# One of three on-chip copies of remainder weights moves from ScalarE to VectorE, and ScalarE's part of the start-up waits for it

## The chip, the cores and the metric

The kernel runs on one core of one Trainium2 chip. Its engines are TensorE (PE in the profile; PEld is its weight load), VectorE (DVE), ScalarE (ACT), GpSimd (POOL) and SyncE (SP). The metric is the device time of one execution in microseconds (us), lower is better.

## The reference

Six cross layers of a recommender network, in bf16, with x0 of 4096 rows and 416 columns, ws of 6 matrices of 416 by 416, and bs of 6 biases:

```
x = x0
for l in range(ws.shape[0]):
    x = x0 * (x @ ws[l] + bs[l]) + x
return x
```

## The kernel before, in words

**Layout.** The state is kept transposed: the 416 columns lie on partitions, the 4096 rows of x0 along the free dimension. 416 is 3 times 128 and a remainder of 32. The three full blocks are in `XM` (three buffers, `XM[0]` holds x0), the remainder in `XR`, where four groups of 512 rows (g = 0 to 3) are stacked on four groups of 32 partitions. The 4096 rows are two halves (s = 0, 1) of four such groups. `WM` holds the weights of the full blocks, `WR` the 32 remainder rows of each layer's weights, copied four times onto the four partition groups, since a matrix product with 32 rows of `XR` needs its weights on the same partitions.

**Loading.** x0 comes from HBM in eight transposing DMAs of 512 rows each, `load_x0t(s, g)` (line 77), all issued by SP one behind another. I call those of the first half T0 to T3. The remainder columns of x0 come as short rows of 64 bytes into `xrem` in four loads (line 82): SP issues the one for s = 0, partitions 0 to 63, between T1 and T2; ACT issues the one for s = 0, partitions 64 to 127 (I call it R), and later the one for s = 1, partitions 0 to 63 (R'). ACT also issues the load of the first layer's `WM` and the load that puts the remainder weights of layers 0 and 1 on partitions 0 to 31 of `WR` (line 85). The three other partition groups of `WR` are filled by on-chip copies: DVE makes those of layer 0 (line 113), ACT those of layer 1 (line 115). The weights of layer 1 in `WR` are first read by `mm_row(1, ...)` (line 214), at the end of the first layer.

**The remainder.** `x0_rem` (lines 160 to 167) turns `xrem` into `XR[0]`: DVE transposes in two parts (line 164), ACT copies the first part into place and DVE the second (line 165), and DVE makes a copy with the two 32-row groups swapped, `XRx` (line 167). For s = 0 this is done for partitions 0 to 63 first, and for partitions 64 to 127 later, behind the first element-wise work (line 272).

**The order of the work.** Every engine executes its instructions in the order in which the program writes them; waits are on semaphores. `first_layer(0)` has PE multiply group g = 0 for the three column blocks (9 matmuls on T0's data), then g = 1 (9 matmuls on T1), then the remainder rows (line 254, 6 matmuls), then g = 2 (9 on T2) and g = 3 (9 on T3), and again remainder rows, which need partitions 64 to 127 of `XR`. Products land in PSUM, whose eight banks are handed out in pairs (`two_banks`); ACT and DVE (lines 189 and 190, 172 and 180) read them out and form the next state. Layers 1 to 4 follow in the loop at line 359, and the last layer produces output rows directly (lines 397 to 457).

The lines that the change touches are 114 and 115; what stands next in ACT's queue is R, and behind it the copy at line 165 and the load R'.

Of the kernel before, what the change touches and what calls it, by code (L numbers as in the profile page):

```python
# [16 lines left out]
def kernel(  # L17
# [7 lines left out]
    nc = tc.nc  # L25
# [7 lines left out]
    NG = 4  # L33
# [20 lines left out]
    WR = const.tile([P, L, D], BF16)  # L54
# [20 lines left out]
    def load_x0t(s, g):  # L75
        c0 = col0(s, g)
        nc.sync.dma_start_transpose(out=XM[0][:, :, c0:c0 + CW], in_=x0[c0:c0 + CW, 0:NK * P])
# [33 lines left out]
        nc.gpsimd.tensor_copy(bsb[32 * g:32 * g + 32, :], bsb[0:R, :])  # L111
    for g in range(1, NG):
        nc.vector.tensor_copy(WR[32 * g:32 * g + 32, 0, :], WR[0:32, 0, :])
    for g in range(1, NG):
        nc.scalar.copy(WR[32 * g:32 * g + 32, 1, :], WR[0:32, 1, :])
    load_x0t(0, 1)
    load_xrem(nc.sync, 0, 0, 64)
    load_xrem(nc.scalar, 0, 64, 128)
# [369 lines left out]
```

## Time and profile before

| quantity | value |
|---|---|
| median of 3 runs | 130.51 us (130.41 to 130.77) |
| profiled execution | 130.41 us |
| its span in the profile | 128.6 us |
| PE busy | 122.5 us, 95% |
| DVE busy | 105.4 us, 82% |
| ACT busy | 84.9 us, 66% |
| POOL busy | 8.9 us, 7% |
| granted TensorE clock | 0.998 of full speed |

The span is the stretch from the first to the last recorded work; 1.8 us of the profiled execution's time lie outside it. Times in the profile are counted from the start of the span. In the timeline a row gives start, duration, engine, source line, operation, output and input, shape and count, and in brackets how long the engine sat idle before and what released it; rows of ACTq and SPq are DMAs being issued by ACT and SP. Waits are given as the total, the number and the longest. In the DMA view a queue's line gives packets, megabytes, and the time that its packets took as a share of 16 DMA engines in the chosen stretch; overlapping packets can bring it over 100%. q1 is the queue of SP's DMAs, q10 that of ACT's.

### The profile page before, as it was taken

The page shows a single profiled execution, that of the slowest core. Times are in us where ns is not written, and L with a number is a line of the kernel's source. Part 1 is how long each engine was busy: PE and PEld are TensorE (multiplying, and loading weights), DVE is VectorE, ACT ScalarE, POOL GpSimd, SP SyncE. Part 2 cuts the span into 40 slices and gives each one's busy share as a digit, 9 for nine tenths or more (in the row PEclk, how much of TensorE's full clock was granted, in tenths as well). Part 3 has the DMA queues.
Part 4 walks back from the last instruction along what each step waited for, and adds up shares of the span by engine and source line. Part 5 has one row for each costly group of instructions (what it writes and reads, how often), then busy time and mean ns, then how long its engine had stood idle before and what let it go on. Part 6 is the DMA issues. An engine that isn't in the chain of part 4 may idle for free. (4 is left out here: it accounts for less than half of the span.)

```text
span 128.6 us, 4040 instructions
## 1 busy us (share of the span) xinstructions
PE 122.5 (95%) x1731; PEld 54.9 (43%) x1731; DVE 105.4 (82%) x192; ACT 84.9 (66%) x97; POOL 8.9 (7%) x29
## 2 busy tenths in 40 slices
PE   6998999999999999999999999999999999999950
PEld 3343344444544443554443444443444454454420
DVE  3358769558697989898989898989898999999990
ACT  2357468693966684966684966584967586676860
POOL 4282000400000000000000000000000050000000
PEclk9999999999999999999999999999999999999999
DMA  3999999999970000000000000000599999999563
GB/s 97 259 178 211 189 208 260 262 329 337 333 219 9 3 0 5 0 5 0 5 0 5 0 5 0 0 5 0 54 200 192 123 165 211 77 344 285 178 208 102
DMA packets 41933, 16.28 MB, mean 127 GB/s; under 512 B 30838, under 2 KB 41916, under 8 KB 41916
## 3 DMA queue, kind: packets, MB, share of 16 engines
q1 hardware_dynamic: 39344, 15.53, 55.3%
q10 hardware_dynamic: 2572, 0.51, 2.2%
q8 instruction: 13, 0.21, 0.7%
q14 instruction: 4, 0.03, 0.1%
HBM read 6.07 MB, written 3.41 MB: 74 GB/s over the span
## 5 line engine op out<-in xcount | busy, mean ns | idle before, releaser
L172 ACT ACTIVATE t<-PS,bM 128x1024 bf16<-128x1024 f32 x56 | 58.1, 1114 | 24.0 <-PE PS L214 22.8
L208 PE MATMUL PS<-XM,WM 128*32 128x512 bf16 x1152 | 65.2, 379 | 0.0
L208 PEld LDWEIGHTS <-WM 128*32 128x32 bf16 x1152 | 29.8, 97 | 33.8 <-issue 5.1
L182 DVE TENSOR_TENSOR t<-t,XM 128x1024 bf16<-128x1024 bf16 x48 | 33.2, 691 | 5.4 <-ACT t L172 5.3
L183 DVE TENSOR_TENSOR XM<-t,XM 128x1024 bf16<-128x1024 bf16 x48 | 33.5, 699 | 2.9
L337 PE MATMUL PS<-WM,XM 128*128 128x416 bf16 x96 | 17.9, 340 | 0.0
L246 PE MATMUL PS<-XM,WM 128*32 128x512 bf16 (+1 forms) x126 | 16.6, 379 | 0.6 <-DMA XM<-in_x_dram 0.5
L405 ACT CAST t<-PS 128x832 bf16<-128x832 f32 x12 | 10.1, 854 | 4.2 <-PE PS L337 2.9
L337 PEld LDWEIGHTS <-XM 128*128 128x128 bf16 x96 | 8.9, 98 | 8.6 <-issue 2.1
L246 PEld LDWEIGHTS <-WM 128*32 128x32 bf16 (+1 forms) x126 | 7.2, 97 | 9.6 <-issue 2.6
L225 PE MATMUL PS<-XM,WM 128*32 128x512 bf16 x120 | 8.2, 379 | 0.0
L407 DVE TENSOR_TENSOR o<-t,XLrows 128x832 bf16<-128x832 bf16 x12 | 7.1, 592 | 0.5
L214 PE MATMUL PS<-XR,WR 32*128 32x512 bf16 x96 | 7.5, 379 | 0.0
L406 DVE TENSOR_TENSOR t<-t,X0rows 128x832 bf16<-128x832 bf16 x12 | 7.0, 585 | 0.0
L180 DVE TENSOR_TENSOR XM<-t,XM 128x1024 bf16<-128x1024 bf16 x7 | 4.8, 691 | 2.8 <-ACT t L172 2.7
L316 POOL COPY XLrows<-scrR 128x512 bf16<-128x512 bf16 x2 | 1.6, 809 | 77.3 <-DMA scrR<-XR 77.3
L196 ACT ACTIVATE t<-PS,bR 128x512 bf16<-128x512 f32 x10 | 6.8, 696 | 0.0
L189 ACT ACTIVATE t<-PS,bM 128x512 bf16<-128x512 f32 x4 | 2.6, 685 | 4.7 <-PE PS L254 4.7
L153 PE MATMUL PS<-warm 128*128 128x512 bf16 (+2 forms) x13 | 4.5, 527 | 1.0 <-DVE warm L87 1.0
L418 ACT CAST t<-PS 128x416 bf16<-128x416 f32 x8 | 4.0, 505 | 1.0 <-PE PS L337 0.6
L225 PEld LDWEIGHTS <-WM 128*32 128x32 bf16 x120 | 3.2, 97 | 3.1
L164 DVE STREAM_TRANSPOSE xrt<-xrem 64x256 bf16<-64x256 bf16 (+1 forms) x5 | 2.2, 477 | 2.3 <-DMA xrem<-in_x_dram 2.3
(45 smaller groups left out, 55.3 us busy)
## 6 DMA issues: line engine op xcount, KB each, us to landing
X0rows<-in_x_dram SPq DMA_DIRECT2D x6, 416.0 KB, 7.7
WM<-in_ws_dram SPq DMA_DIRECT2D x5, 312.0 KB, 5.5
out_dram<-o SPq DMA_DIRECT2D x3, 416.0 KB, 4.3
out_dram<-o SPq DMA_DIRECT2D x6, 208.0 KB, 2.1
X0rows<-in_x_dram SPq DMA_DIRECT2D x1, 832.0 KB, 9.6
out_dram<-o SPq DMA_DIRECT2D x8, 104.0 KB, 1.7
WR<-in_ws_dram SPq DMA_DIRECT2D x4, 104.0 KB, 4.8
WM<-in_ws_dram ACTq DMA_DIRECT2D x1, 312.0 KB, 3.4
```

The costliest lines, as they stand in the source:

```text
L172: nc.scalar.activation(t[:], pt.rearrange("p a b -> p (a b)"), ACT.Identity, bias=bM[:, m, l:l + 1], scale=1.0)
L182: nc.vector.tensor_tensor(out=t, in0=t, in1=x0c, op=ALU.mult)
L183: nc.vector.tensor_tensor(out=nxt[:, m, c0:c0 + 2 * CW], in0=t, in1=cur[:, m, c0:c0 + 2 * CW], op=ALU.add)
L196: nc.scalar.activation(tr[:, 0:CW], pr, ACT.Identity, bias=bR[:, l:l + 1], scale=1.0)
L208: nc.tensor.matmul(pts[g // 2][32 * q:32 * q + 32, g % 2, :], lhsT=WM[:, l, k, 128 * m + 32 * q:128 * m + 32 * q + 32], rhs=cur[:, k, c0:c ...
L214: nc.tensor.matmul(pts[g // 2][:, g % 2, :], lhsT=WR[32 * g:32 * g + 32, l, 128 * m:128 * m + 128], rhs=curR[32 * g:32 * g + 32, CW * s:CW ...
L225: nc.tensor.matmul(pr[32 * g:32 * g + 32, :], lhsT=WM[:, l, k, NK * P:D], rhs=cur[:, k, c0:c0 + CW], start=False, stop=(k == NK - 1), tile ...
L246: nc.tensor.matmul(pt[q0:q1, gl, :], lhsT=WM[:, 0, k, 128 * m + q0:128 * m + q1], rhs=cur[:, k, c0:c0 + CW], start=(first and k == 0), sto ...
L337: nc.tensor.matmul(py[g // 2][:, g % 2, 0:D], lhsT=xL[:, k, q_cols(q, g)], rhs=WM[:, LL, k, :], start=(first and k == 0), stop=((not first ...
L405: nc.scalar.copy(tv, py[h][:, :, 0:D])
L406: nc.vector.tensor_tensor(out=tv, in0=tv, in1=X0rows[:, b0:b0 + 5:4, :], op=ALU.mult)
L407: nc.vector.tensor_tensor(out=o, in0=tv, in1=XLrows[:, b0:b0 + 5:4, :], op=ALU.add)
```

## The change

DVE, having made its three copies of layer 0, makes the copy of layer 1 onto partitions 32 to 63. ACT makes the other two, and reads them from partitions 32 to 63, where DVE has just written, and no longer from partitions 0 to 31. So ACT's first copy waits for DVE, and what stands behind it in ACT's queue, the load R first, is issued after that wait. PE, SP and POOL have the same instructions in the same order as before.

```diff
     for g in range(1, NG):
         nc.vector.tensor_copy(WR[32 * g:32 * g + 32, 0, :], WR[0:32, 0, :])
-    for g in range(1, NG):
-        nc.scalar.copy(WR[32 * g:32 * g + 32, 1, :], WR[0:32, 1, :])
+
+    nc.vector.tensor_copy(WR[32:64, 1, :], WR[0:32, 1, :])
+    for g in range(2, NG):
+        nc.scalar.copy(WR[32 * g:32 * g + 32, 1, :], WR[32:64, 1, :])
     load_x0t(0, 1)
     load_xrem(nc.sync, 0, 0, 64)
     load_xrem(nc.scalar, 0, 64, 128)
```

## The prediction

> **What bounds the kernel now.** First the page's busy line, then TensorE's waits:
>
> ```profile
> PE 122.5 (95%) x1731; PEld 54.9 (43%) x1731; DVE 105.4 (82%) x192; ACT 84.9 (66%) x97; POOL 8.9 (7%) x29
> ```
>
> ```profile
> PE PS L246 <- DMA XM<-in_x_dram: 0.5, 2, 0.4
> ```
>
> PE is busy nearly all the span, and its only waits for data are for the transposing loads of x0 in the first layer. So a start-up edit reaches the end only through the time at which PE gets through these. The timeline of PE at the start:
>
> ```profile
> 5.71 4.05 PE L246 MATMUL PS<-XM,WM 128*128 128x512 bf16 x18 [0.17 <-DMA XM<-in_x_dram]
> 9.69 0.60 PE L254 MATMUL PS<-XR,WR 32*128 32x512 bf16 x4
> 9.97 0.39 PE L254 MATMUL PS<-XRx,WR 32*128 32x512 bf16 x2
> 10.73 4.23 PE L246 MATMUL PS<-XM,WM 128*128 128x512 bf16 x18 [0.37 <-DMA XM<-in_x_dram]
> ```
>
> The 18 matmuls at 10.73 are nine on T2 and nine on T3. They take 4.23 us where the first 18 take 4.05: the single records show starts every 0.216 us from 10.73 to 12.45, and then a tenth at 12.86, 0.19 late. So T3 holds PE too, though the waits do not list it. SP issues these loads:
>
> ```profile
> 4.93 0.66 SPq L82 DMA_DIRECT2D xrem<-in_x_dram  x1
> 5.64 7.66 SPq L77 DMA_TRANSPOSE XM<-in_x_dram  x4
> ```
>
> T2 is issued at 5.64, T3 at 7.79. The DMA view of a stretch that holds each issue alone gives 5.0 us to landing for both: 10.64 and 12.8, just ahead of the starts at 10.73 and 12.86. T3's landing is the last gate; later transposes do not hold PE.
>
> **What is beside T2 and T3.** ACT's and DVE's rows around the edit, and the flight of R:
>
> ```profile
> 5.95 0.54 ACT L115 COPY WR<-WR 32x416 bf16<-32x416 bf16 x1 [2.07 <-DMA WR<-in_ws_dram]
> 5.96 0.63 ACTq L82 DMA_DIRECT2D xrem<-in_x_dram  x1
> 6.51 1.10 ACT L115 COPY WR<-WR 32x416 bf16<-32x416 bf16 x2
> 8.64 0.62 ACT L165 COPY XR<-xrt 64x256 bf16<-64x256 bf16 x1 [1.04 <-DVE xrt L164]
> ```
>
> ```profile
> 5.95 0.84 DVE L113 COPY WR<-WR 32x416 bf16<-32x416 bf16 x3 [0.53 <-DMA WR<-in_ws_dram]
> 8.17 0.76 DVE L164 STREAM_TRANSPOSE xrt<-xrem 64x256 bf16<-64x256 bf16 x2 [1.38 <-DMA xrem<-in_x_dram]
> 12.32 0.77 DVE L164 STREAM_TRANSPOSE xrt<-xrem 64x256 bf16<-64x256 bf16 x2
> ```
>
> ```profile
> xrem<-in_x_dram ACTq DMA_DIRECT2D x1, 64.0 KB, 4.5
> ```
>
> R's issue does not wait for the copies to execute, only for the wait of the first one. R lands at 5.96 + 4.5 = 10.5 and is first read at 12.32. The DMA view from 8.2 to 9.7, then from 14.5 to 15.3 where SP's queue runs alone:
>
> ```profile
> q1 hardware_dynamic: 1113, 0.28, 86.5%
> q10 hardware_dynamic: 1039, 0.07, 48.7%
> ```
>
> ```profile
> q1 hardware_dynamic: 892, 0.23, 126.8%
> ```
>
> R's packets run from 8.2 to 9.7, inside T2, and take 48.7% of 1.5 us, 0.73 us of all 16 engines. SP's queue moves 742 packets per us beside them and 1115 alone.
>
> **The change, part by part.**
>
> *The copies.* DVE's copies of this size start every 0.29 us and take 0.26. The fourth runs from 6.81 to 7.07, in the 1.38 us that DVE sits idle until 8.17: cost nothing; without that cover, 0.29 us on DVE. ACT loses one copy of 0.54. Its first now starts at about 7.14 (DVE's end plus the 0.07 seen between the transpose at 8.17 and the copy at 8.64), its second ends at 8.25, 0.39 ahead of the copy at 8.64, which waits for DVE anyway. The copied weights are first read by PE at 25.2. POOL's wait for the copies at line 136 is at 23, also covered.
>
> *R.* Its issue moves from 5.96 to 7.15, ending at 7.78, still ahead of R' at 8.65. No SP instruction waits for it until 18.6. With its old flight of 4.5 it lands at 11.65, 0.67 ahead of its reader; beyond that DVE would slip, but PE first reads the result at 14.89, 1.0 after the swapped copy ends (13.89). So up to 1.6 us of further lateness cost PE nothing.
>
> *T2.* R's packets began 2.25 us after issue, those of R' (8.65, packets from 11.1) 2.45 after. R now begins at 9.4 to 9.6, behind T2. T2's 1113 packets alone take 1.0 us in place of 1.5, so it lands up to 0.5 earlier, near 10.2. Without that wait PE starts the block 0.31 after the last pair of remainder rows (the step seen from 15.12 to 15.43), at 10.28.
>
> *T3.* This decides, and the trace has no row of R beside T3. From 10.28, nine matmuls bring PE to 12.22; two PSUM pairs are freed only by DVE's row at 10.21 (1.41 us, two instructions), which holds the fourth and seventh matmul to about 11.03 and 11.69 and the tenth to 12.33. The most to be had is 12.86 - 12.33 = 0.52 us. How much comes depends on T3's landing. For a gain: T3 can follow T2 up to 0.5 earlier, and from 9.7 to 10.3 the engines' share is 0.93 against 1.27 at full flow, room for 0.2 us of R's 0.73. Against: the remaining 0.53 must go somewhere, and if T3 gains no start, it delays T3. So T3 moves by -0.5 to +0.5, or to +0.73 if no room is used. The eight transposes took 4.2 to 5.3 us; at 4.6, between T3's 5.0 and the least, T3 lands at 12.4. I take that value, because the stretch that T2 gives back (0.5) lies directly ahead of T3 on the same queue, and T3's slow phase has room for more.
>
> **The sum.** PE's tenth matmul from 12.86 to 12.44: -0.42. Copies, R's reader, POOL, SP: 0. Behind 12.86 PE waits for no load, so the shift reaches the tail, whose chain of waits is DVE's, fed by PE. The profiled execution was 130.41 us (span 128.6, 1.8 outside), which gives 129.99; it was the lowest of the runs, 0.10 under their median, so 130.09 as a median, 130.1 rounded. A difference under 0.3% (0.39 us) is about what a measurement of this kernel can tell from no change.
>
> **A rule on queues.** The Trainium skill (DMA: Bandwidth & Descriptors, Issuing engines are not separate DMA queues) says that transfers issued from any engine run on the same 16 DMA engines and interleave. The rows at 8.2 to 9.7 agree (86.5% beside 48.7%). By that rule alone R's work is only moved, T3 ends when it did, and the sum is nothing: the first rival.
>
> **Rivals.**
> *The wait only moves from T2 to T3.* T2 is early, R fills exactly the time that T2 gave back, T3 lands at 12.8 as before and PE waits there the whole 0.6. For it: the engines run over 1.2 in most stretches from 4 on, so R's 0.73 us has few holes to fall into; T3's issue (7.79, after T2's) is not moved. Against: the stretch at 0.93. It gives 130.4 to 130.5; with shifts of T3 up to 0.39 either way it is the case of no change.
> *T3 is delayed.* R's 1024 packets come between T2 and T3 or inside T3, and T3, which is the last gate, pays them with nothing hidden: at most 0.73, PE's tenth matmul at 13.6, 131.2 us; with the room of 0.2 used, 0.53, 131.0. It is slower as soon as T3 lands past 12.8, and measurably so past 13.2. For it: the same 64-byte rows issued by SP at 4.93 ran with the engines at a share of 0.60 from 6.5 to 7.5, so they can cost more than their packets' time. Against: T2 beside R still took 5.0 us, as T0 and T1 took 5.0 and 4.9.
> *The change does not do what it says:* R is held in the DMA engines until 8.2 anyway, 1.05 us behind its new issue (the first WM load, issued at 0.72, had its first packets at 1.8); nothing moves. 130.5. This goes with no change.
>
> **How the numbers follow.** Both waits shrink: 0.40. The wait only moves, or nothing moves: 0.36. T3 delayed: 0.24, some of it by less than 0.5. The range runs from 129.9 (the ceiling of 0.52 from the median, with 0.1 for run to run) to 130.95 (a delay of 0.44), which leaves out half of the last case and little else. For the forecast alone it is 129.95 to 130.2.
>
> **What would show it.** In the profile after: a DVE copy at 6.8, ACT's copies and R's issue at about 7.15; q10's packets from 9.4 on; T2 issued at 5.64 as before but landing at 10.1 to 10.3, no wait of PE at 10.73; T3 landing at 12.4 and the tenth matmul of the block at 12.4 to 12.5; the same distance from there to the end. It is wrong if T3 lands at 12.8 or later, if R's packets still begin at 8.2, or if a wait appears at DVE's second transpose that reaches the remainder rows at 14.9.

## The result and the profile after

The changed kernel takes 130.96 us (median of 17 runs, 130.43 to 131.37), the kernel before 130.34 us beside it (17 runs, 129.98 to 130.77). The ratio is 1.0048, 95% interval 1.0035 to 1.0062: slower by 0.62 us. The forecast was 130.1 with a range up to 130.95. The profiled execution of the change took 131.04 us with a span of 129.3 us, against 130.41 and 128.6 before.

ACT's and DVE's part of the edit went as forecast. Timelines of the changed kernel, ACT first, then DVE:

```profile
7.17 0.54 ACT L117 COPY WR<-WR 32x416 bf16<-32x416 bf16 x1 [3.29 <-DVE WR L115]
7.18 0.62 ACTq L82 DMA_DIRECT2D xrem<-in_x_dram  x1
7.73 0.54 ACT L117 COPY WR<-WR 32x416 bf16<-32x416 bf16 x1
```

```profile
6.88 0.26 DVE L115 COPY WR<-WR 32x416 bf16<-32x416 bf16 x1
```

R is issued at 7.18, 1.22 later than before. What became of T2 and T3 stands in the DMA view, for one stretch around T2's issue at 5.70 and one around T3's at 7.65 (the last number is the time to landing):

```profile
XM<-in_x_dram SPq DMA_TRANSPOSE x1, 4.1
```

```profile
XM<-in_x_dram SPq DMA_TRANSPOSE x1, 5.6
```

In the kernel before, the row for T2 (stretch from 5.5) and the one for T3 (from 7.78) read the same:

```profile
XM<-in_x_dram SPq DMA_TRANSPOSE x1, 5.0
```

T2 was to gain and did, 5.0 to 4.1. T3 was to gain too and lost, 5.0 to 5.6, though it was issued 0.14 earlier. PE's waits and timeline:

```profile
PE PS L248 <- DMA XM<-in_x_dram: 1.1, 2, 0.8
```

```profile
10.14 0.39 PE L256 MATMUL PS<-XRx,WR 32*128 32x512 bf16 x2
10.46 2.12 PE L248 MATMUL PS<-XM,WM 128*128 128x512 bf16 x9
13.34 2.10 PE L248 MATMUL PS<-XM,WM 128*128 128x512 bf16 x8 [0.76 <-DMA XM<-in_x_dram]
```

The wait ahead of T2's nine matmuls is gone; the one ahead of T3's is 0.76 us, and they start at 13.34 where they started at 12.86 before: 0.48 us lost. A second loss is far away, where the output rows begin. DVE's timeline there, before and after:

```profile
107.26 0.58 DVE L406 TENSOR_TENSOR t<-t,X0rows 128x832 bf16<-128x832 bf16 x1
107.93 0.59 DVE L407 TENSOR_TENSOR o<-t,XLrows 128x832 bf16<-128x832 bf16 x1
```

```profile
107.73 0.58 DVE L408 TENSOR_TENSOR t<-t,X0rows 128x832 bf16<-128x832 bf16 x1
108.77 0.59 DVE L409 TENSOR_TENSOR o<-t,XLrows 128x832 bf16<-128x832 bf16 x1 [0.46 <-issue]
```

The shift grows from 0.47 to 0.84 between two neighbouring instructions, with an idle of 0.46 that the profile puts on no work ("issue"). From there DVE runs without a break to the end.

### The profile page after: what moved, and what is told of

Same layout as the page of the kernel before. It is cut to its first block, busy times and chain, and to the rows that moved or that the text cites. A ratio compares the mean times of both kernels' runs of the same rounds, so it can differ in the third digit from the quotient of the medians.

```text
span 129.3 us, 4039 instructions
## 1 busy us (share of the span) xinstructions
PE 122.3 (95%) x1730; PEld 54.7 (42%) x1731; DVE 105.8 (82%) x193; ACT 84.4 (65%) x96; POOL 9.2 (7%) x29
## 5 line engine op out<-in xcount | busy, mean ns | idle before, releaser
L192 DVE SCALAR_TENSOR_TENSOR XM<-PS,bM,XM 128x512 bf16<-128x512 f32 x4 | 2.9, 746 | 1.3 <-PE PS L256 1.2
```

## The experiments

U0 to U3 are the transposes of the second half. "Tenth" is the start of the tenth of the 18 matmuls on T2 and T3; "37th" the start of PE's first matmul on U0; "rest" the time from there to the end of DVE's last output add. The last four columns are read from the one profiled execution of each kernel; the ratio is to the kernel before, from runs on the same chip. c1's profile is of an execution of 130.56 us, 0.9 over its median.

| kernel | ratio (95% interval) | T2, T3 in flight | tenth | 37th | rest |
|---|---|---|---|---|---|
| before | 1 | 5.0, 5.0 | 12.86 | 15.43 | 110.26 |
| the change | 1.0048 (1.0035 to 1.0062) | 4.1, 5.6 | 13.34 | 15.91 | 110.62 |
| e1 | 1.0012 (0.9998 to 1.0025) | 5.0, 4.7 | 12.48 | 15.05 | 110.59 |
| e2 | 1.0058 (1.0041 to 1.0074) | 4.0, 5.4 | 13.12 | 15.70 | 110.59 |
| e3 | 1.0009 (0.9995 to 1.0023) | 4.4, 5.0 | 12.78 | 15.36 | 110.33 |
| e4 | 1.0041 (1.0023 to 1.0058) | 4.4, 4.3 | 13.29 | 15.87 | 110.22 |
| e5 | 1.0035 (1.0023 to 1.0047) | 5.2, 5.1 | 12.68 | 15.26 | 110.58 |
| e6 | 1.0016 (1.0000 to 1.0032) | 4.5, 5.2 | 12.90 | 15.48 | 110.34 |
| e7 | 1.0034 (1.0021 to 1.0048) | 4.6, 4.6 | 12.30 | 14.88 | 110.96 |
| e8 | 1.0002 (0.9987 to 1.0016) | 5.2, 4.2 | 12.78 | 15.36 | 110.23 |
| c1 | 0.9967 (0.9946 to 0.9988) | 4.3, 4.9 | 12.86 | 15.44 | 110.48 |
| c2 | 0.9983 (0.9967 to 1.0000) | 4.9, 5.2 | 12.95 | 15.52 | 110.23 |
| c3 | 1.0000 (0.9988 to 1.0012) | 4.4, 4.5 | 12.22 | 14.91 | 110.55 |
| c4 | 0.9967 (0.9956 to 0.9978) | 4.9, 4.5 | 12.34 | 14.92 | 110.25 |

**The parts of the change.** e1 keeps the moved copy and takes away ACT's wait for DVE; e2 keeps the copies and takes over R's delay alone.

e1:

```diff
-        nc.scalar.copy(WR[32 * g:32 * g + 32, 1, :], WR[32:64, 1, :])
+        nc.scalar.copy(WR[32 * g:32 * g + 32, 1, :], WR[0:32, 1, :])
```

> The copies as in the change (one on VectorE, two on ScalarE), but ScalarE's two read partitions 0 to 31, so that they wait for the load and not for VectorE, and R is issued near 5.96 as before. Theory 1 (the time of R's issue is the whole cost: R's 64-byte rows are served between T2 and T3 and T3 pays): T3 lands at 12.8, PE's tenth matmul on T2/T3 starts at 12.86, time as before within 0.15%. Theory 2 (the copies themselves cost: VectorE's fourth copy, or one more instruction in its stream): the time stays 0.4 to 0.5% over before, although T3 lands at 12.8.

e2, against the kernel before (`spare` is a new tile):

```diff
+    nc.vector.tensor_copy(spare[32:64, 0:D], WR[0:32, 1, :])
     for g in range(1, NG):
         nc.scalar.copy(WR[32 * g:32 * g + 32, 1, :], WR[0:32, 1, :])
+    nc.scalar.copy(spare[32:64, D:D + 1], spare[32:64, 0:1])
```

> ScalarE makes all three copies as before; VectorE makes a copy of the same size into a spare tile, and a one-column ScalarE copy that reads it holds R back to about 7.2. Theory 1: T2 lands near 9.8, T3 near 13.3, the tenth matmul at 13.3, time 0.4 to 0.5% over before, as in the change. Theory 2: the spare copy on VectorE costs the same as the moved one, so the time is over before too, but with T3 at 12.8.

With R back at 5.78 (e1), T2 and T3 are back near their old flights and most of the loss is gone; with R at 7.07 and every copy on its old engine (e2), T2 is early and T3 late by nearly the same amounts as in the change, and the time is the change's within the intervals. So the late front comes with R's issue, as theory 1 says. But the last column shows a second cost, the one that theory 2 named as one more instruction in DVE's stream: 110.6 in the change, e1 and e2, whatever the front, and 110.2 to 110.3 in before, e3 and e4. e1 carries that cost too and still lies at before's time, so its front is better than before's, by more than theory 1 allows.

**The instruction that moves a pause.** DVE's instruction records show 0.407 us between the dispatch of the first output add (107.93, the 191st instruction recorded on DVE) and the next record, with nothing waited for; the add's own 0.59 us hide it. With one more instruction ahead, the same pause falls in front of that add, as in the change: 0.46 idle. e5 and e6 add one two-column memset, in DVE's idle time at 2 us:

```diff
     nc.vector.transpose(out=pick[1][:], in_=pick[0][:])
+    nc.vector.memset(spare[:], 0.0)
```

> The kernel before with one more VectorE instruction, a two-column memset of a spare tile at the start, where VectorE is idle. Theory A (a change of place in VectorE's instruction stream: the sequencer pauses 0.41 us after its 191st recorded instruction, and one more ahead of it moves the pause from behind a running operation to ahead of the first output add): the idle of 0.46 before the first output add appears, the front is as before (T3 at 12.8), and the time is 0.35 us, 0.25 to 0.3%, over before. Theory B (that idle comes from the late front or from the transfers of the tail): no idle, time as before within 0.15%.

> The changed kernel with the same spare memset. Theory A: the pause falls between two waits ahead of the first output add and is hidden, the idle of 0.46 goes, and 0.3 to 0.37 us come back: 0.1 to 0.25% over before, with T3 still landing at 13.1 to 13.3 and the tenth matmul at 13.1 to 13.4. Theory B: idle and time stay, 0.45 to 0.6% over before.

The tail of e5, then of e6 (DVE timelines):

```profile
107.06 0.58 DVE L408 TENSOR_TENSOR t<-t,X0rows 128x832 bf16<-128x832 bf16 x1
108.10 0.59 DVE L409 TENSOR_TENSOR o<-t,XLrows 128x832 bf16<-128x832 bf16 x1 [0.46 <-issue]
```

```profile
107.40 0.58 DVE L410 TENSOR_TENSOR t<-t,X0rows 128x832 bf16<-128x832 bf16 x1
108.08 0.59 DVE L411 TENSOR_TENSOR o<-t,XLrows 128x832 bf16<-128x832 bf16 x1
```

A memset that computes nothing needed costs 0.35% when it is one (e5, 0.47 us between the medians) and gives back 0.32 points of the change's 0.48% when it is the second (e6). Theory A is shown: the pause has a fixed place in DVE's instruction stream, and what stands there decides whether it costs.

What is R's part? e6's 0.16% is not R's alone, since e6 has the moved copy too. Kernels that differ only in which partitions ACT's copies read, and so in R's issue, give it: the change against e1 0.36 points, e6 against c2 (e1 with the memset, below) 0.33. Each has some 0.2 either way. So R's delay costs about as much as the pause, some 0.45 us each. The moved copy without either lies 0.17% below before (c2, at the edge of its interval), which fits the sum being only 0.48%.

e6's front missed what was expected of it: T3 lands at 12.86 there, 0.4 earlier than in the change, with the same order of issues. Landings with one order of issues scatter by that much and more (12.14 in e1, 12.91 in c2). So the table's front is read over several kernels, not from one pair.

**Where R stands, and what it is made of.** e3 moves R behind ACT's first remainder copy, e4 ahead of ACT's copies; e7 lets R bring its 64 KB in 64 pieces of 1 KB, of other columns of x0, and leaves out the remainder columns that belong there.

e3 and e4, against before (the line is taken out of its place and put in):

```diff
     x0_rem(0, 0, 64, (nc.scalar.copy, nc.vector.tensor_copy))
+    load_xrem(nc.scalar, 0, 64, 128)
     load_xrem(nc.scalar, 1, 0, 64)
```

```diff
+    load_xrem(nc.scalar, 0, 64, 128)
     for g in range(1, NG):
         nc.scalar.copy(WR[32 * g:32 * g + 32, 1, :], WR[0:32, 1, :])
```

> The kernel before, with R moved behind ScalarE's copy of the first remainder half, so that it is issued at 8.65 directly ahead of R', after most of T3's issue. Theory 1 (service in the order of issue): R's packets come behind T3's, T2 lands at 9.8, T3 at 12.0 to 12.4, the tenth matmul at 12.33 to 12.45, time 0.3 to 0.4% below before. Rival (the engines only share their time, whoever is first): R's 0.73 us falls on T3 again, T3 lands at 13.0 to 13.5, time 0.2 to 0.5% over before. In both R lands by 13.5, late for VectorE's second transpose but ahead of PE at 14.9.

> The kernel before, with R issued ahead of ScalarE's copies, at about 3.9, during T1's issue. Theory 1: R is served ahead of the first remainder half and of T2, T1 lands up to 0.6 later (7.6, PE needs it at 7.7), the first half's rows land up to 0.7 later (8.8) and hold PE's remainder rows at 9.7 to 10.3, T2 and T3 land as before or up to 0.3 earlier; time within 0.3% of before. Rival (sharing): T2 and T3 are both free of R and land 0.3 to 0.5 earlier, time 0.2 to 0.4% below before.

e7, against the change:

```diff
-    load_xrem(nc.scalar, 0, 64, 128)
+    nc.scalar.dma_start(xrem[0][64:128].rearrange("p t r -> p (t r)"),
+                        x0[1024:2048, :].rearrange("(p t) d -> p (t d)", t=16)[:, 0:512])
```

> The changed kernel, but R brings the same 64 KB as 64 pieces of 1 KB in place of 1024 pieces of 64 bytes, issued at the same time; what it brings are other columns of x0, so the remainder of half of the first 2048 rows is computed from wrong numbers. Theory 1a (the number of R's pieces is what T3 waits for): T2 lands near 9.7, T3 at 12.0 to 12.4, the tenth matmul at 12.4 to 12.5, time 0.3% below to 0.1% over before, with the idle of 0.46 in the tail kept. Theory 1b (any load that stands between T2 and T3 holds T3 back): T3 at 13.1 to 13.3, time as in the change, 0.5% over before.

R's first packets follow its issue by 1.7 to 3.2 us, and come within the last transpose that SP had issued ahead, behind all the others: issued at 2.36 (e4, earlier than I expected, since no instruction ahead held it) they begin at 5.6, behind T0 and within T1; at 5.96 (before) at 8.2, within T2; at 7.18 (change) at 8.8, as T2 ends; at 8.56 (e3) at 10.96, as T3 ends. The transpose beside R, or the one behind it, pays. In e4 it is T1, 6.5 us in flight in place of 4.9, and the time is 0.41% over before, where theory 1 had 0.3 at most:

```profile
8.74 2.10 PE L246 MATMUL PS<-XM,WM 128*128 128x512 bf16 x9 [0.96 <-DMA XM<-in_x_dram]
```

How T3 pays is in the DMA view from 9.0 to 9.7 (packets, MB, share of 16 engines), for before, the change and e7:

```profile
q1 hardware_dynamic: 439, 0.10, 71.6%
q10 hardware_dynamic: 659, 0.04, 65.0%
```

```profile
q10 hardware_dynamic: 599, 0.04, 58.0%
q1 hardware_dynamic: 50, 0.01, 10.8%
```

```profile
q1 hardware_dynamic: 473, 0.11, 88.7%
q10 hardware_dynamic: 75, 0.06, 36.8%
```

Before, R's packets run beside T2's last and T3's first and fill the engines together (137%). In the change T2 is nearly done, R's small pieces come almost alone, no faster than before, and SP's queue moves 50 packets, although T3 was issued 1.35 us ahead of this stretch: the share is 69%, half of what it was. In e7, with the same bytes at the same place, SP's queue moves 473, T2's last 200 and T3's first 240.

Landings blur this, so T3's last packet tells more. A transpose is 1536 packets of 256 bytes, and counted so, T3's last one starts at 11.72 to 11.92 in the four kernels with R at 7.1 to 7.2 in small pieces (the change, e2, e6, c1), and at 10.95 to 11.36 in the ten others: 11.36 in before, 11.29 in e7. So T3 waits neither for bytes nor for the engines' time, but for the service of R's 1024 pieces ahead of it and beside it: theory 1a, as far as T3 goes. Which unit serves them so, no run tells. The rest of e7's early landing (12.12 against 13.29 in the change) is not R's doing: from last packet to landing it took 0.83 us there and 1.51 in the change.

That stretch, from last packet to landing, also accounts for e3, which met neither of its two expectations (T3 at 12.0 to 12.4, or at 13.0 to 13.5). T3's last packet came at 11.24, as in the kernels that spare it, but T3 landed at 12.68 and the time stayed as before. It is 1.3 to 1.6 us in the six profiles in which a load of small pieces (R', in e3 R) passes within 0.6 to 0.8 us right as T3 ends (before, the change, e2, e3, e5, c2), and 0.5 to 1.1 in the eight others. Why, no run shows.

In time, e7 missed its expectation (0.1% over before at most): it lies at 0.34%, and the 0.14 points to the change are within the intervals. Its tenth matmul is 0.56 ahead of before's, yet it takes as long as e5, which has the same pause. PE's timeline shows why:

```profile
14.88 1.47 PE L249 MATMUL PS<-XM,WM 128*128 128x512 bf16 x6
16.50 0.81 PE L249 MATMUL PS<-XM,WM 128*128 128x512 bf16 x3
```

Six matmuls on U0, and then PE stands until U1 lands at 16.45. In the kernel before U1 landed at 16.55 and PE came to it at 15.43 + 6 x 0.216 = 16.73: U1 is the next gate, 0.18 behind.

**R', and versions that are faster.** e8 and c3 issue R' later, with DVE's stream as before. e8's edit (c3 also moves R, to the place that R' leaves):

```diff
             x0_rem(0, 64, 128, (nc.scalar.copy, nc.vector.tensor_copy))
+            load_xrem(nc.scalar, 1, 0, 64)
...
     x0_rem(0, 0, 64, (nc.scalar.copy, nc.vector.tensor_copy))
-    load_xrem(nc.scalar, 1, 0, 64)
```

> The kernel before, with R' (the load of the second half's first remainder part) issued behind ScalarE's second remainder copy, near 12.8 and not 8.65; R stays at 5.96. If R', whose packets run at the end of T3's, holds T3's landing back: T3 lands 0.7 after its last packet in place of 1.4, at 12.1 to 12.4, and the tenth matmul starts at 12.65 to 12.7 (nine matmuls after T2's wait), time 0.1 to 0.15% below before. If R' has no part in it: T3 at 12.8, time as before. R' lands near 17.2 and may hold VectorE's transpose at 17.35 up to 0.3.

> The kernel before with R behind T3 (8.65, as in e3) and R' behind the second remainder copy (near 13.4). In-order service: T2 at 9.6 to 10.1, T3 at 11.9 to 12.3 (4.2 to 4.6 after its issue), U1, the sixth transpose, at 15.4 to 16.0, so that PE's next gate is free too; the time is 0.1 to 0.25% below before, held back where the TensorE clock comes up late. Sharing alone: T3 at 12.7, time as before.

With R' gone from its end, T3 takes 4.2 (e8) and 4.5 (c3, c4) and lands at 11.6 to 12.1; with R' there it takes 4.7 to 5.2 (before, e1, e3, e5, c2). So R' does hold T3, though c4 and e1 are only 0.2 apart. The time of e8 and c3 stays as before all the same. In e8 T2, which has R beside it, lands at 10.65, so the nine matmuls on it put the tenth at 12.6 at best. In its profiled execution PE came later still, at 10.80, since its first 18 matmuls take 4.77 us (4.04 in c4), the first of them 0.35 to 0.43 apart until 7.1, and then 0.216:

```profile
5.56 4.77 PE L246 MATMUL PS<-XM,WM 128*128 128x512 bf16 x18
```

```profile
5.70 4.04 PE L250 MATMUL PS<-XM,WM 128*128 128x512 bf16 x18 [0.28 <-DMA XM<-in_x_dram]
```

In c3 R lands at 12.95, DVE's second transpose waits 0.66 for it, and PE's remainder rows wait in turn:

```profile
12.97 0.77 DVE L163 STREAM_TRANSPOSE xrt<-xrem 64x256 bf16<-64x256 bf16 x2 [0.66 <-DMA xrem<-in_x_dram]
PE PS L253 <- DVE XR L164: 0.3, 1, 0.3
```

The last three put the findings together. c1 is the change with the spare memset and R' late, c2 is e1 with the memset, c4 is c2 with R' late.

> The changed kernel with the spare VectorE memset (as in e6) and R' issued behind ScalarE's second remainder copy (as in e8). If R' lengthens T3 here too: T2 lands at 9.6 to 10.2, T3 at 12.3 to 12.6 in place of 12.9 to 13.3, no idle ahead of the first output add, time 0.0 to 0.2% below before. If T3's delay is all R's: T3 stays at 12.9 to 13.3, time 0.1 to 0.2% over before as in e6.

> The copies as in the change but reading partitions 0 to 31 (R near 5.9, as in e1), with the spare VectorE memset. If the pause in VectorE's stream was all that e1 paid: no idle ahead of the first output add and 0.3 to 0.45 us less than e1, 0.15 to 0.25% below before. If moving a copy has a cost or gain of its own, or e1 owed its low time to chance: within 0.1% of before.

> c2 with R' issued behind the second remainder copy. Gains add: T3 lands at 11.6 to 12.0, time 0.2 to 0.35% below before. If T2's wait is by then the gate (T2 at 10.5 to 10.65 with R beside it): the time equals that of c2.

c1 and c4 beat the kernel before by 0.33%, with intervals clear of 1; c2 gains 0.17%, at the edge of its interval. c2 against e1 is the pause once more (110.23 against 110.59, 0.29 points). In c4 T2 takes 4.9 and T3 4.5, the tenth matmul starts at 12.34 and U1 lands at 16.10, ahead of PE at 14.92 + 1.30. What stays open: putting R' late is worth 0.5 points on top of e6 (c1), 0.16 on top of c2 (c4) and nothing on top of before (e8), so the gains do not add, and single profiles don't say why; c1's runs also spread most, from 129.53 to 130.81. Nor is it shown why the moved copy alone, with R early, is slightly faster than before (e1 less its pause, c2).

## Why the prediction was wrong

*The copies* were timed right (6.88, 7.17 and 8.27 against 6.81, 7.14 and 8.25) and costed wrong. "Cost nothing" counted an instruction by the idle time around it. It also pushed every later DVE instruction one place on, and the pause of 0.41 us with it: the term is 0.47 us by e5, where it stood as 0 because DVE sat idle.

*R's reader, POOL and SP* held: R landed at 11.53 against 11.65 forecast, 0.84 ahead of its reader.

*T2* was right in direction and low in size: it landed at 9.80, where 10.2 was forecast. R's packets began at 8.8, 1.66 after the issue and not 2.25 to 2.45, which were read from issues with more work queued ahead.

*T3* is the step that failed. The working gave T3 the 0.5 us that T2 gave back and room in its slow phase; the value taken was a flight of 4.6, and it took 5.6. The argument treated R as 0.73 us of engine time, to be put wherever engines were free. The runs show R's pieces served ahead of T3 and beside it at a rate of their own, at a share of 69% where it had been 137%, and T3's last packet 0.4 us later for it, 0.5 later than with pieces of 1 KB (e7). The warning was at hand, in the row quoted for that rival: the same small pieces, issued by SP, ran nearly alone from 6.5 to 7.5 at a share of 0.60.

*The ceiling of 0.52 us* was wrong as well. "Behind 12.86 PE waits for no load" is true of the trace before, but U1 was only 0.18 us behind PE. A gain of 0.42 at T3 alone would have been cut to about that, and the forecast with it. The hold by PSUM pairs, from which the ceiling came, is not borne out either: in c3 PE starts this block at 10.24 and its tenth matmul at 12.22, nine steps of 0.22 on and ahead of the 12.33 that was to be the earliest.

*The rivals.* T3 delayed (0.24) was what happened; the 0.48 us that PE lost in the profile, and the 0.45 that R's delay costs by the pairs of kernels, are just under the rival's bounds of 0.53 to 0.73. That its time, 131.0, was met as well is in part luck: the pause adds as much again, which no rival had, and part of it is missing from the sum because the kernel with the moved copy alone is faster than before, at the edge of its interval and for no reason that the runs show. By the rule on queues (the Trainium skill, DMA: Bandwidth & Descriptors, Issuing engines are not separate DMA queues) the two queues' transfers interleave on the same engines, which the trace shows (58.0% beside 10.8%); what the prediction drew from it, that T3 would end when it did, the trace does not bear out: it landed 0.48 later.

## What to carry to other kernels

Before a small-piece load is moved "out of the way" of one transfer, look at which transfer is issued next, and whether that one is the last gate: here the load left the transfer for which the wait was longer and held up the one that came last. Count an added instruction also as a shift of the whole stream behind it: an idle with no releaser at one place of a stream is worth searching for once; here one dummy instruction brought it and a second one took it away. When a gate moves earlier, check the slack of the next gate of the same kind ahead of promising the gain.

## What the runs showed of the hardware

**A pause of 0.41 us in DVE's instruction stream**, at the same instruction count in every kernel: behind the 190th or 191st recorded instruction, hidden or exposed by what stands there. The Trainium skill (Runtime: NRT & Kernel Launch, Instruction fetch mechanics) says that instructions are refilled in blocks of 16 KiB and that crossing a boundary is mostly hidden. The profile's queue q8, of kind "instruction", does move 13 packets of that size, one every 4 to 10 us from 21 us on; the next one follows the start of the pause by 0.4 us in e7 and by 1.3 in before, so the trace does not tie it to the pause. That the pause is such a crossing is an inference; it was not hidden where it stood ahead of the first output add: 0.47 us of the time in e5.

**TensorE's rate at the start differs from execution to execution.** Matmuls of 512 columns start 0.43 us apart until some point, and 0.216 behind it: from 4.3 us (e7, c2) to 7.1 us (e8). The Trainium skill (TensorE: Matmul & The Clock Gate, Part 1) describes a free-running activity window of about 3.4 us for this and in one place lets the point vary by 500 ns either way; the spread of 2.9 us here is larger, though within one window. That the clock is the cause these traces don't show: their column of the granted clock reads 1.00 in e8 from 3.0 to 7.5 us. The first 18 matmuls took 4.77 us in e8 and 4.04 in c4, so the front of one profile is compared with another's only with this in view.

**Landing follows the last packet by very different times**: 0.7 us for T2 in the change, 1.5 for T3 there, with R' running at its end, 1.8 for T1 in e4, with R at its end, and 0.5 for T3 in e8, with nothing of ACT's queue there.
